# Attention, then routed experts, on one core: gathered token rows turned by a DMA on SyncE's queue, five places for expert weights, three evacuation tiles in the experts' first stage

## The chip, the cores and the metric

The kernel runs on one core of one Trainium2 chip, in one launch. The metric is the device time of one execution in microseconds (us); the figure for a kernel is the median of its runs.

## The reference

An attention over 8 batches of 8 heads (sequence 1152, head width 64) whose queries are averaged in pairs, so that 576 query rows per head remain, is followed by a routed two-layer network. All inputs and outputs are float32.

```
q_pool = q.reshape(B, H, S // 2, 2, D).mean(axis=3)
scores = scale * np.matmul(q_pool, k.transpose(0, 1, 3, 2))     # scale = 1/8
attn = exp(scores - max) / sum
x = (attn @ v), heads side by side                              # 4608 tokens x 512
for e in range(8):
    mask = domain_id == e
    out[mask] = np.maximum(x[mask] @ w1[e], 0.0) @ w2[e]         # 512 -> 1024 -> 512
```

## The kernel before

**Attention.** Two heads form a pair; there are 32 pairs of 12 steps, 384 steps in all (`for t in range(NST + 4)`, L849). A step computes 432 columns of key-by-query scores for both heads on TensorE (`score`, L578; matmul L587), and ScalarE takes their exponential into fp16 (`expo`, L593; L599). The weighted sums of values follow some steps later (`av`, L603; L610), and VectorE divides by the sums into the batch's tile `xb` (`evac`, L617; L624). A finished batch is written by DMA, row by row in token order, to a scratch tensor `x_tok` in memory (`put_x`, L634; nine pieces of 32 to 96 rows each, L639). All of these go on SyncE's queue (SP), except that of the last batch the pieces with odd `i` go on ScalarE's. The q loads (L99) are on SP too; the k and v loads, which cast to fp16 (L112, L121), the weight loads (L485 to L494), the gathers of token rows (L648) and the scatters of output rows (L504) are all on GpSimd's queue (POOL).

**Routing.** While the attention runs, VectorE works out each token's place in its expert's list. Every expert has room for 640 rows, five tiles of 128. The places are laid out so that an expert's tile 0 holds rows of the first two batches alone, tile 1 of the first four, tile 2 of the first six; tiles 3 and 4 may hold rows of any batch (`KO`, `IB`, `get_x` L653). So three tiles of every expert can be gathered before the last batch is done. There are 8 x 5 = 40 tiles.

**Expert tiles during the attention.** A tile costs four transposes of its gathered rows (`turn`, L747: L751, copied out by VectorE L756), 32 matmuls of the first stage (`up`, L763, relu on VectorE L768) and 8 of the second (`down`, L776, copied out L782). A planner (L907 to L921) hands out these pieces: each step has 769 ns (`STEP`); what the attention does in it is charged with C_S, C_AV, C_TK and C_TQ (370, 315, 460 and 420 ns), and a piece (240 ns for a turn, 216 ns for each of 4 matmuls up or 1 down) is issued when the running debt stays under 190 ns (`LAG`). No piece is begun by the planner from step NST - 5 = 379 on; at step NST + 1 a tile that was begun is finished (L896). `HELD` experts have their weights loaded during the attention, at the steps of `WANT`, into the places of `wpool`. `want` (L799) lists the gathers of the attention and the earliest step of each; 20 gathered tiles have room (`NFX`).

**Experts after the attention.** `plan_runs` (L831) makes a list of runs (expert, first tile, end). Before: expert 3 tiles 0 to 2; experts 0, 1, 2 from their first undone tile to 5; expert 3 tiles 3 and 4; experts 4 to 7, five tiles each. `first_xt` (L838) turns the first run's rows on TensorE (L843, L846). For each run (L1051), `stage1` (L996) multiplies the turned rows by the first weights, 128 hidden rows at a time (`f` = 0 to 7, L1010), and evacuates with relu, even `f` on ScalarE (L1015), odd `f` on VectorE (L1017). `stage2` (L1024) multiplies by the second weights (L1031) and copies out (L1037, L1039); then a scatter takes the 128 rows to the output. Between the tiles of `stage2`, `turn_tile` (L982; L985) transposes the next run's tiles on TensorE, and VectorE and ScalarE take turns in copying them out (L989, L991). When an expert is finished, the next unheld expert's weights are loaded into its place (L1066). In runs of up to four tiles two values of `f` share one PSUM tile, a half each:

```
            if m > 512:
                hp_ = hps.tile([P, 1024], FP32, name="hp")
            elif f % 2 == 0:
                hb_ = hps.tile([P, 1024], FP32, name="hp")
                hp_ = hb_[:, 0:512]
            else:
                hp_ = hb_[:, 512:1024]
```

The matmuls, copies and DMAs of each engine are executed in the order in which this program issues them. A block behind L1076, for experts with over 640 tokens, does not run on these inputs.

Of the kernel before, what the change touches and what calls it, by code (L numbers as in the profile page):

```python
# [9 lines left out]
P = 128  # L10
# [9 lines left out]
def kernel(  # L20
# [34 lines left out]
    NFX = 20  # L55
# [4 lines left out]
    wpool = ctx.enter_context(tc.tile_pool(name="wpool", bufs=4))  # L60
# [10 lines left out]
    idp = att.enter_context(tc.tile_pool(name="idp", bufs=2))  # L71
    lop = att.enter_context(tc.tile_pool(name="lop", bufs=6))
# [21 lines left out]
    def load_q(p, gate=False):  # L94
        b, h = p // HP, 2 * (p % HP)
        q2 = lds.tile([QP, 2, NJ, 2 * D], FP32, name="q2")
        mark(q2[0:1, 0, 0, 0:1], gate)
        for lo, hi in ((0, 1), (1, 2)) if p < 2 else ((0, 2),):
            nc.sync.dma_start(  # L99
                q2[:, lo:hi, :, :].rearrange("p h j d -> p h (j d)"),  # L100
                q[b, h + lo : h + hi].rearrange("h (p r) d -> p h (r d)", p=QP),
            )
        loaded.setdefault(p, {})["q2"] = q2
# [23 lines left out]
    k32 = perm.tile([P, 2, NC, D], FP32, name="k32")  # L127
# [12 lines left out]
    load_q(1)  # L140
# [23 lines left out]

    load_v(0)
    load_k(1)
    load_dom()
    keep_warm(17)
    make_identity(nc, ident[:, :])
# [258 lines left out]
    def id_group(g, i):  # L428
        if i == 0:
            gst["eq"] = idp.tile([P, GC, NH], F16, name="eq")  # L430
            nc.vector.tensor_tensor(
                out=gst["eq"][:, :, :],
                in0=hif[:, g * GC : (g + 1) * GC].unsqueeze(2).broadcast_to([P, GC, NH]),
                in1=iol[:, 0:NH].unsqueeze(1).broadcast_to([P, GC, NH]), op=ALU.is_equal,
            )
            gst[g] = idp.tile([P, GC, 2, NH], F16, name="hi2")
        else:
            nc.vector.tensor_tensor(
                out=gst[g][:, :, i - 1, :], in0=gst["eq"][:, :, :],
                in1=dig[:, i - 1, g * GC : (g + 1) * GC].unsqueeze(2).broadcast_to([P, GC, NH]),  # L440
                op=ALU.mult,
            )

    def id_lo(c):
        gst["lo", c] = lop.tile([P, P], F16, name="lo1")
# [95 lines left out]
    def new_kq(p):  # L541
        if p not in kq:
            kq[p] = work.tile([P, KW], F16, name="kq")
# [90 lines left out]
    def put_x(b, i):  # L634
        for lo, hi in zip(CUT, CUT[1:]):
            i_, m = (0, lo) if lo < 64 else (1 + (lo - 64) // P, (lo - 64) % P)
            if i_ == i:
                j, p0 = divmod(lo, QP)
                (nc.scalar if b == B - 1 and i % 2 else nc.sync).dma_start(  # L639
# [20 lines left out]
    xs = {}  # L660
    wqueue = []
# [10 lines left out]
    HELD = 4  # L672
    WANT = [66, 100, 134, 230]
# [34 lines left out]
    keep_warm(6)  # L708
# [3 lines left out]
    def rest_k():  # L712
        keep_warm(2)
# [3 lines left out]
        keep_warm(3)  # L717
# [23 lines left out]
    tiles, turned = [], []  # L741

    def add_tile(e, i):
# [3 lines left out]
        def turn():  # L747
            turned.append((e, i))
            mt = mpsum.tile([P, ND, P], F16, name="m")
            for cc in range(ND):  # L750
                nc.tensor.transpose(  # L751
                    mt[:, cc, :], in_=xs[e, i][:, cc * P : (cc + 1) * P], identity=ident16[:, :]
                )
            h0["xt"] = fill.tile([P, ND, P], F16, name="xt0")
            h0["h"] = fill.tile([P, NF, P], F16, name="h0")
            nc.vector.tensor_copy(h0["xt"][:, :, :], mt[:, :, :])  # L756

        def up(f):
            if f % 4 == 0:
                h0["m"] = mpsum.tile([P, 4, P], FP32, name="m")  # L760
# [12 lines left out]
        def down(f):  # L773
            if f == 0:
                h0["o"] = mpsum.tile([P, 512], FP32, name="m")
# [13 lines left out]
        fb.blocks.append(([turn], 240, 1, False, h0))  # L789
        fb.blocks.append(([lambda f=f: up(f) for f in range(4)], 216, 1, True, h0))  # L790
# [3 lines left out]
    for e, i in [(e, i) for i in range(2) for e in range(3)] + [  # L794
        (e, i) for e in range(3, HELD) for i in range(2)
    ]:
        add_tile(e, i)

    want = [(e, 0, 114) for e in range(3)] + [(e, 1, 212) for e in range(3)]  # L799
    want += [(e, i, 212) for e in range(3, E) for i in range(2)]  # L800
    want += [(e, 2, 308) for e in [3, 0, 1, 2] + list(range(HELD, E))]
# [27 lines left out]
    xt = {0: perm.tile([P, ND, CAP], F16, name="xt_first")}  # L829

    def plan_runs():  # L831
        early = [e for e in range(3, HELD) if done.get(e, 0) < NA]
        runs.extend((e, done.get(e, 0), NA) for e in early)
        runs.extend((e, done.get(e, 0), NTC) for e in range(3))
        runs.extend((e, NA if e in early else done[e], NTC) for e in range(3, HELD))
        runs.extend((e, 0, NTC) for e in range(HELD, E))

    def first_xt():  # L838
        e, i0, i1 = runs[0]
        for i in range(i0, i1):  # L840
            mt = mpsum.tile([P, ND, P], F16, name="m")
            for cc in range(ND):
                nc.tensor.transpose(  # L843
                    mt[:, cc, :], in_=xs[e, i][:, cc * P : (cc + 1) * P], identity=ident16[:, :]
                )
            nc.vector.tensor_copy(xt[0][:, :, (i - i0) * P : (i - i0 + 1) * P], mt[:, :, :])  # L846

    debt = 0
    for t in range(NST + 4):  # L849
# [17 lines left out]
        if t == 0:  # L867
            rest_k()
        if t in (1, 2, 3):
            keep_warm(3)  # L870
# [25 lines left out]
        if t == NST + 1:  # L896
# [3 lines left out]
            first_xt()  # L900
        if main and want and t >= want[0][2] and t >= last_get + 5 and not (t in later) and not mmq and not rq:
            e, i, _ = want[0]
            if len(got) < NFX or list(got)[len(got) - NFX] in turned:
                get_x(fxs, e, i)
                got[e, i] = last_get = t
                want.pop(0)
        while main:  # L907
            if fb.cur is None:
# [3 lines left out]
                if not b_[3] and t < got.get(b_[4]["xs"], NST) + 14:  # L912
# [51 lines left out]
    while wqueue:  # L964
# [4 lines left out]
        tc.tile_pool(name="hps", bufs=2, space=bass.MemoryType.PSUM, reuse_waits="tile")  # L969
# [4 lines left out]
    xps = ctx.enter_context(  # L974
        tc.tile_pool(name="xps", bufs=2, space=bass.MemoryType.PSUM, reuse_waits="tile")
    )
    tb = ctx.enter_context(tc.tile_pool(name="tb", bufs=2, reuse_waits="tile"))
    xsb = ctx.enter_context(tc.tile_pool(name="xsb", bufs=10, reuse_waits="tile"))
    xov = ctx.enter_context(tc.tile_pool(name="xov", bufs=1, reuse_waits="tile"))
    ob = ctx.enter_context(tc.tile_pool(name="ob", bufs=8, reuse_waits="tile"))  # L980

    def turn_tile(xt, x_, i):  # L982
        ps = xps.tile([P, ND, P], F16, name="xp")
        for cc in range(ND):
            nc.tensor.transpose(  # L985
                ps[:, cc, :], in_=x_[:, cc * P : (cc + 1) * P], identity=ident16[:, :]
            )
        if i % 2 == 0:
            nc.vector.tensor_copy(xt[:, :, i * P : (i + 1) * P], ps[:, :, :])  # L989
        else:  # L990
            nc.scalar.copy(xt[:, :, i * P : (i + 1) * P], ps[:, :, :])  # L991
# [4 lines left out]
    def stage1(w1h, xt, m, at=None):  # L996
        hT = tb.tile([P, NF, CAP], F16, name="hT")
        for f in range(NF):

            if m > 512:  # L1000
                hp_ = hps.tile([P, 1024], FP32, name="hp")
            elif f % 2 == 0:
                hb_ = hps.tile([P, 1024], FP32, name="hp")
                hp_ = hb_[:, 0:512]
            else:
                hp_ = hb_[:, 512:1024]
# [17 lines left out]
    def stage2(w2h, hT, n, ids, between=()):  # L1024
        between = list(between)
        for i in range(n):
            for _ in range(-(-len(between) // (n - i))):
                between.pop(0)()
# [22 lines left out]
    for k_, r in enumerate(runs):  # L1051
# [6 lines left out]
        get = lambda: fetch(k_ + 2)  # L1058
        h = stage1(wts[e][0], xt[k_], n * P, {1: get, 4: get, 6: get} if n < NTC else {1: get, 3: get, 5: get})
        btw = []  # L1060
        if k_ + 1 < len(runs):
            nx = xt[k_ + 1] = new_xt()
            en, j0, j1 = runs[k_ + 1]
            btw = [lambda i=i: turn_tile(nx, xs[en, j0 + i], i) for i in range(j1 - j0)]
        stage2(wts[e][1], h, n, lambda i, c=e * NTC + i0: gid[:, c + i : c + i + 1], btw)
# [10 lines left out]
    with tc.If(anyov > 0):  # L1076
# [9 lines left out]
        for e in range(E):  # L1086
# [4 lines left out]
            with tc.For_i(0, nt, 1) as j:  # L1091
# [13 lines left out]
                turn_tile(xto, xo, 0)  # L1105
# [30 lines left out]
```

The softmax here doesn't subtract the row's maximum and nothing guards it: scores larger than these inputs give would overflow.

## Time and profile before

| | |
|---|---|
| median of 4 runs | 473.52 us (471.48 to 474.54) |
| the profiled execution's own time | 473.74 us |
| its span in the profile | 471.7 us |
| ScalarE, first and last exponential | 9.32 us, end 317.05 us |
| last value matmul of the attention, end | 317.56 us |
| last matmul of all, end | 463.96 us |
| busy: TensorE, ScalarE, VectorE, GpSimd | 442.6, 347.6, 228.0, 160.4 us |

Times in the profile are in us from the start of the span unless marked ns. A row of groups names line, engine, operation, what it writes and reads, shapes and count; then busy time, mean ns of one, the idle time of the engine just before, and what ended that idle time. PE is TensorE's matmuls, PEld its weight loads, DVE VectorE, ACT ScalarE, SP SyncE's queue. The end of a matmul is modelled, so a group of matmuls is shown to end slightly after the next group has begun.

### The profile page before, as it was taken

Reading aid. Unit: us, or ns where it says so; the run is one execution under the profiler, and the core shown is the slowest. Engines: PE = TensorE matmul, PEld = TensorE weight load, DVE = VectorE, ACT = ScalarE, POOL = GpSimd, SP = SyncE. Lnnn points to the kernel's source line nnn. Section 1 sums busy time; section 2 is a strip of 40 time slices with the busy share of each in tenths; the row PEclk is TensorE's granted clock in tenths of the full one; section 3 lists DMA queues with packets and bytes.
Section 4 is the critical chain, followed back from the end, with each engine's and each line's share of the span. In section 5 each row is a group of like instructions: output and inputs, shape, how many; then the busy total and the mean of one; then the engine's idle time right before and its main releaser. Section 6 shows DMA issues by size and latency. Waiting matters only on the chain.

```text
span 471.7 us, 13280 instructions
## 1 busy us (share of the span) xinstructions
PE 442.6 (94%) x5683; PEld 313.6 (66%) x5683; DVE 228.0 (48%) x572; ACT 347.6 (74%) x459; POOL 160.4 (34%) x271
## 2 busy tenths in 40 slices
PE   7999999999999999999999999996888879999993
PEld 4777777777877877877787787773444445555551
DVE  4498778776555554655455554532223223232230
ACT  3999999999999999999999999981222223223220
POOL 4311141222511304564512441004335675532413
PEclk9999999999999999999999999998999999999998
DMA  9995699999999789599998676003219999912202
GB/s 205 219 243 93 119 242 223 182 259 198 157 243 243 114 190 206 99 195 265 241 154 206 140 124 143 1 25 107 78 68 165 212 218 228 236 46 84 89 20 98
DMA packets 48904, 75.23 MB, mean 159 GB/s; under 512 B 5567, under 2 KB 35008, under 8 KB 48834
## 3 DMA queue, kind: packets, MB, share of 16 engines
q0 software_dynamic: 35056, 50.05, 55.6%
q1 hardware_dynamic: 13186, 23.83, 18.8%
q8 instruction: 46, 0.75, 0.7%
q10 hardware_dynamic: 592, 0.39, 0.3%
q14 instruction: 24, 0.20, 0.1%
HBM read 95.46 MB, written 15.21 MB: 235 GB/s over the span
## 4 chain that ended last, share of the span: by engine, by line
ACT 54%; PE 23%; issue 10%; POOL 6%; DMA 3%; DVE 1%; POOLq 1%; SPq 0%; ACTq 0%
ACT e L599 52%; PE s L587 6%; PE hp L1010 6%; PE op L1031 4%; POOL out_dram L504 4%; PE acc L610 3%; DMA w2h<-in_moe_w_dram 3%; ACT hT L1015 2%; POOL xs L648 1%; PE m L763 1%; PE tp L550 1%; DMA x_tok<-xb 1%; PE xp L985 1%; SPq L639 0%; PE acc L161 0%
## 5 line engine op out<-in xcount | busy, mean ns | idle before, releaser
L599 ACT ACTIVATE e<-s 128x864 f16<-128x864 f32 x384 | 305.4, 893 | 2.8 <-PE s L587 2.4
L587 PE MATMUL s<-qz,kq 128*128 128x432 f16 (+2 forms) x1152 | 202.9, 284 | 4.1 <-ACT e L599 2.0
L610 PEld LDWEIGHTS <-e 128*128 128x128 f16 x2880 | 120.4, 97 | 24.9 <-DVE xb L624 8.2
L610 PE MATMUL acc<-v,e 128*128 128x65 f16 x2880 | 134.2, 193 | 0.3 <-ACT e L599 0.3
L587 PEld LDWEIGHTS <-kq 128*128 128x128 f16 x1152 | 97.5, 97 | 28.5 <-issue 8.1
L504 POOL DMA_INDIRECT out_dram<-osb,gid x40 | 40.1, 1002 | 101.5 <-ACT osb L1037 46.3
L1010 PE MATMUL hp<-xt,w1h 128*128 128x128 f16 (+3 forms) x384 | 57.7, 303 | 8.9 <-ACT hT L1015 8.9
L648 POOL DMA_INDIRECT xs<-x_tok,grow x40 | 41.6, 1040 | 71.1 <-DVE xs L92 55.2
L112 POOL DMA_DIRECT2D vs<-in_v_dram x32 | 23.9, 745 | 116.9 <-DVE v L529 55.5
L1031 PE MATMUL op<-w2h,hT 128*128 128x512 f16 x272 | 63.4, 379 | 0.0
L1010 PEld LDWEIGHTS <-w1h 128*128 128x128 f16 x416 | 35.9, 98 | 41.2 <-issue 17.5
L1015 ACT ACTIVATE hT<-hp 128x384 f16<-128x384 f32 (+2 forms) x36 | 20.7, 574 | 49.6 <-PE hp L1010 42.9
L1017 DVE TENSOR_SCALAR hT<-hp 128x384 f16<-128x384 f32 (+2 forms) x36 | 23.8, 661 | 65.2 <-PE hp L1010 65.2
L571 DVE COPY qz<-tp 64x576 f16<-64x576 f16 x62 | 28.2, 455 | 54.5 <-PE tp L564 50.5
L1037 ACT COPY osb<-op 128x512 f32<-128x512 f32 x21 | 12.3, 586 | 55.7 <-PE op L1031 50.0
L1031 PEld LDWEIGHTS <-hT 128*128 128x128 f16 x272 | 25.4, 98 | 25.2
L623 DVE RECIPROCAL rr<-acc 128x10 f32<-128x10 f32 x32 | 7.1, 221 | 46.6 <-PE acc L610 46.5
L520 DVE TENSOR_TENSOR qp<-q 96x768 f16<-96x768 f32 x31 | 29.3, 946 | 0.0
L624 DVE TENSOR_TENSOR xb<-acc,rr 128x640 f16<-128x640 f32 x32 | 26.4, 824 | 1.1
L1039 DVE COPY osb<-op 128x512 f32<-128x512 f32 x13 | 9.0, 692 | 35.5 <-PE op L1031 29.6
L121 POOL DMA_DIRECT2D k<-in_k_dram x31 | 23.3, 752 | 7.1 <-DVE q L92 4.1
L554 DVE COPY kq<-tp 128x1024 f16<-128x1024 f16 x31 | 21.2, 684 | 3.2 <-PE tp L550 3.2
(134 smaller groups left out, 324.7 us busy)
## 6 DMA issues: line engine op xcount, KB each, us to landing
q<-in_q_dram SPq DMA_DIRECT2D x30, 576.0 KB, 9.3
vs<-in_v_dram POOLq DMA_DIRECT2D x32, 288.0 KB, 6.1
k<-in_k_dram POOLq DMA_DIRECT2D x31, 288.0 KB, 8.5
w1h<-in_moe_w_dram POOLq DMA_DIRECT2D x16, 512.0 KB, 9.0
w2h<-in_moe_w_dram POOLq DMA_DIRECT2D x16, 512.0 KB, 12.1
x_tok<-xb SPq DMA_DIRECT2D x23, 96.0 KB, 4.1
x_tok<-xb SPq DMA_DIRECT2D x22, 64.0 KB, 4.6
q<-in_q_dram SPq DMA_DIRECT2D x4, 288.0 KB, 7.1
```

Of the source, the lines that this page charges most:

```text
L112: nc.gpsimd.dma_start(vs[:, :, :, :], v[b, h : h + 2].rearrange("h (p c) d -> p h c d", p=P))
L504: ins = nc.gpsimd.indirect_dma_start(out=dst[:, :], out_offset=bass.IndirectOffsetOnAxis(ap=ap, axis=0), in_=src, in_offset=None, **kw,)
L520: nc.vector.tensor_tensor(out=qp[:, :, :, :].rearrange("p j h d -> p h j d"), in0=q2[:, :, :, 0:D], in1=q2[:, :, :, D : 2 * D], op=ALU.add,)
L571: nc.vector.tensor_copy(qz[p % 2][r][lo : lo + 64, :], mt[lo : lo + 64, P : P + Sp])
L587: nc.tensor.matmul(s[:, r, o : o + n], lhsT=kq[p][:, c * P : (c + 1) * P], rhs=qz[p % 2][r][:, q0 : q0 + n], start=True, stop=True,)
L599: nc.scalar.activation(e_[:, :, o : o + W], st.pop(t)[:, :, 0:W], AF.Exp, bias=0.0, scale=0.0625)
L610: nc.tensor.matmul(acc[p][:, h, i * (D + 1) : (i + 1) * (D + 1)], lhsT=e_[:, h, o + QO[i] : o + QO[i] + P], rhs=v16[p % NV][:, c, h, 0 : D ...
L624: nc.vector.tensor_tensor(out=xb[b][:, :, 2 * hp * D : 2 * (hp + 1) * D].rearrange("p i (h d) -> p h i d", h=2), in0=a[:, :, :, 0:D], in1= ...
L648: nc.gpsimd.indirect_dma_start(out=dst, out_offset=None, in_=x_dram[0 : 1 + nb * Sp, :], in_offset=bass.IndirectOffsetOnAxis(ap=ap, axis=0),)
L1010: nc.tensor.matmul(hp_[:, lo : lo + n], lhsT=w1h[:, cc, f * P : (f + 1) * P], rhs=xt[:, cc, lo : lo + n], start=cc == 0, stop=cc == ND - 1,)
L1015: nc.scalar.activation(hT[:, f, 0:m], hp_[:, 0:m], AF.Relu)
L1031: nc.tensor.matmul(op_[:, :], lhsT=hT[:, f, i * P : (i + 1) * P], rhs=w2h[:, f, :], start=f == 0, stop=f == NF - 1,)
```

## The change

The turning of gathered rows goes from TensorE to a transposing DMA on SP's queue (`flip_x`), both for the tiles computed during the attention and for all runs after it. A tile of the attention is flipped 8 steps or more after its gather, and its first matmul may come 6 steps after the flip. `first_xt` is gone: the first run's three tiles are flipped during the attention into `xf`, which lies on the same place as the prologue's `k32`. After the attention, the flips of run k + 1 are issued on SP ahead of `stage1` of run k. The tiles planned for the attention are tiles 0, 1 and 2 of experts 0, 1 and 2.

`wpool` has five places, and the fifth expert's weights are loaded from step 290 on. The list of runs now begins with tiles 0 to 2 of expert 3 and of expert 4; then come experts 0, 1, 2, the rest of 3 and of 4, and experts 5 to 7. There are 14 places for rows gathered in the attention (before 20) and 16 for those after it (before 10).

`stage1` takes a PSUM tile of its own for every `f`, out of three; the two tiles that took the transposes are gone. All pieces of the last batch go to `x_tok` on SP. In the prologue, the second pair's q load and the load of `domain_id` are issued later, the identity is made before the first v and k loads, some filler matmuls (`keep_warm`) go, and the rest of the first keys is turned one step later. The routing's intermediate tiles (`eq`, `hi2`, `lo1`) use the buffers of the expert tiles in `fill`, `lo1` as eight slices of one tile, and `kq` has a pool of its own, with two buffers as before.

```diff
@@ -52,12 +52,12 @@
...
-    NFX = 20
+    NFX = 14
...
-    wpool = ctx.enter_context(tc.tile_pool(name="wpool", bufs=4))
+    wpool = ctx.enter_context(tc.tile_pool(name="wpool", bufs=5))
@@ -68,8 +68,7 @@
...
-    idp = att.enter_context(tc.tile_pool(name="idp", bufs=2))
-    lop = att.enter_context(tc.tile_pool(name="lop", bufs=6))
+    kqs = att.enter_context(tc.tile_pool(name="kqs", bufs=2))
@@ -95,7 +94,7 @@
...
-        for lo, hi in ((0, 1), (1, 2)) if p < 2 else ((0, 2),):
+        for lo, hi in ((0, 1), (1, 2)) if p == 0 else ((0, 2),):
@@ -124,7 +123,8 @@
...
-    k32 = perm.tile([P, 2, NC, D], FP32, name="k32")
+    xf = perm.tile([P, ND * CAP], F16, name="xf")
+    k32 = xf[:, 0 : 4 * NC * D].bitcast(FP32).rearrange("p (h c d) -> p h c d", h=2, c=NC)
@@ -137,7 +137,6 @@
...
-    load_q(1)
@@ -162,11 +161,10 @@
...
+    keep_warm(17)
+    make_identity(nc, ident[:, :])
     load_v(0)
     load_k(1)
-    load_dom()
-    keep_warm(17)
-    make_identity(nc, ident[:, :])
@@ -636,7 +636,7 @@
...
                 j, p0 = divmod(lo, QP)
-                (nc.scalar if b == B - 1 and i % 2 else nc.sync).dma_start(
+                nc.sync.dma_start(
@@ -658,6 +658,10 @@
...
+
+    def flip_x(dst, e, i):
+        nc.sync.dma_start_transpose(dst, xs[e, i][:, :])
+
...
     def want_weights(e):
...
-    HELD = 4
-    WANT = [66, 100, 134, 230]
+    HELD = 5
+    WANT = [66, 100, 134, 220, 290]
@@ -705,16 +709,16 @@
...
-    keep_warm(6)
+    load_q(1, True)
+    load_dom()
+    keep_warm(5)
...
     def rest_k():
-        keep_warm(2)
         kb = wps[:, 0, :].bitcast(F16)
         turn_k32(kb, CUTK, NC)
         nc.vector.tensor_copy(kq[0][:, CUTK * P : NC * P], kb[:, 0 : (NC - CUTK) * P])
-        keep_warm(3)
 
@@ -738,26 +742,27 @@
...
         def turn():
-            turned.append((e, i))
-            mt = mpsum.tile([P, ND, P], F16, name="m")
-            for cc in range(ND):
-                nc.tensor.transpose(
-                    mt[:, cc, :], in_=xs[e, i][:, cc * P : (cc + 1) * P], identity=ident16[:, :]
-                )
             h0["xt"] = fill.tile([P, ND, P], F16, name="xt0")
-            h0["h"] = fill.tile([P, NF, P], F16, name="h0")
-            nc.vector.tensor_copy(h0["xt"][:, :, :], mt[:, :, :])
+            flip_x(h0["xt"][:, :, :], e, i)
+            h0["t"] = now[0]
...
         def up(f):
+            if f == 0:
+                h0["h"] = fill.tile([P, NF, P], F16, name="h0")
+                begun.append((e, i))
+                turned.append((e, i))
             if f % 4 == 0:
@@ -786,19 +791,17 @@
...
-        fb.blocks.append(([turn], 240, 1, False, h0))
-        fb.blocks.append(([lambda f=f: up(f) for f in range(4)], 216, 1, True, h0))
+        turns.append((e, i, turn))
+        fb.blocks.append(([lambda f=f: up(f) for f in range(4)], 216, 1, False, h0))
         fb.blocks.append(([lambda f=f: up(f) for f in range(4, 8)], 216, 1, True, h0))
         fb.blocks.append(([lambda f=f: down(f) for f in range(NF)], 216, 1, True, h0))
 
-    for e, i in [(e, i) for i in range(2) for e in range(3)] + [
-        (e, i) for e in range(3, HELD) for i in range(2)
-    ]:
+    for e, i in [(e, i) for i in range(NA) for e in range(HELD - 2)]:
         add_tile(e, i)
...
-    want = [(e, 0, 114) for e in range(3)] + [(e, 1, 212) for e in range(3)]
-    want += [(e, i, 212) for e in range(3, E) for i in range(2)]
-    want += [(e, 2, 308) for e in [3, 0, 1, 2] + list(range(HELD, E))]
+    want = [(e, 0, 114) for e in range(HELD - 2)] + [(e, 1, 212) for e in range(HELD - 2)]
+    want += [(e, i, 212) for e in range(HELD - 2, E) for i in range(2)]
+    want += [(e, 2, 308) for e in [3, 4, 0, 1, 2, 5, 6, 7]]
@@ -826,24 +829,14 @@
...
     runs = []
-    xt = {0: perm.tile([P, ND, CAP], F16, name="xt_first")}
+    xt = {0: xf[:, :].rearrange("p (n c) -> p n c", n=ND)}
+    first = [(HELD - 2, i) for i in range(NA)]
 
     def plan_runs():
-        early = [e for e in range(3, HELD) if done.get(e, 0) < NA]
-        runs.extend((e, done.get(e, 0), NA) for e in early)
-        runs.extend((e, done.get(e, 0), NTC) for e in range(3))
-        runs.extend((e, NA if e in early else done[e], NTC) for e in range(3, HELD))
+        runs.extend((e, 0, NA) for e in (HELD - 2, HELD - 1))
+        runs.extend((e, done.get(e, 0), NTC) for e in range(HELD - 2))
+        runs.extend((e, NA, NTC) for e in (HELD - 2, HELD - 1))
         runs.extend((e, 0, NTC) for e in range(HELD, E))
-
-    def first_xt():
@@ -864,10 +857,8 @@
...
-        if t == 0:
+        if t == 1:
             rest_k()
-        if t in (1, 2, 3):
-            keep_warm(3)
@@ -897,19 +888,25 @@
...
             plan_runs()
-            first_xt()
...
+
+        if turns and t >= got.get(turns[0][:2], NST) + 8 and len(tiles) - len(turns) <= len(begun):
+            turns.pop(0)[2]()
+        if first and t >= got.get(first[0], NST) + 8:
+            e, i = first.pop(0)
+            turned.append((e, i))
+            flip_x(xt[0][:, :, i * P : (i + 1) * P], e, i)
...
                 b_ = fb.blocks[0]
-                if not b_[3] and t < got.get(b_[4]["xs"], NST) + 14:
+                if not b_[3] and t < b_[4].get("t", NST) + 6:
@@ -966,29 +963,15 @@
...
     hps = ctx.enter_context(
-        tc.tile_pool(name="hps", bufs=2, space=bass.MemoryType.PSUM, reuse_waits="tile")
+        tc.tile_pool(name="hps", bufs=3, space=bass.MemoryType.PSUM, reuse_waits="tile")
...
-    xps = ctx.enter_context(
-        tc.tile_pool(name="xps", bufs=2, space=bass.MemoryType.PSUM, reuse_waits="tile")
-    )
...
-    xsb = ctx.enter_context(tc.tile_pool(name="xsb", bufs=10, reuse_waits="tile"))
+    xsb = ctx.enter_context(tc.tile_pool(name="xsb", bufs=16, reuse_waits="tile"))
@@ -996,14 +979,7 @@
...
         for f in range(NF):
-
-            if m > 512:
-                hp_ = hps.tile([P, 1024], FP32, name="hp")
-            elif f % 2 == 0:
-                hb_ = hps.tile([P, 1024], FP32, name="hp")
-                hp_ = hb_[:, 0:512]
-            else:
-                hp_ = hb_[:, 512:1024]
+            hp_ = hps.tile([P, 1024], FP32, name="hp")
@@ -1055,14 +1028,14 @@
...
         if k_ == len(runs) - 1:
             nc.gpsimd.drain()
-        get = lambda: fetch(k_ + 2)
+        else:
+            xt[k_ + 1] = new_xt()
+            en, j0, j1 = runs[k_ + 1]
+            for j in range(j0, j1):
+                flip_x(xt[k_ + 1][:, :, (j - j0) * P : (j - j0 + 1) * P], en, j)
+        get = lambda: fetch(len(runs))
         h = stage1(wts[e][0], xt[k_], n * P, {1: get, 4: get, 6: get} if n < NTC else {1: get, 3: get, 5: get})
-        btw = []
-        if k_ + 1 < len(runs):
-            nx = xt[k_ + 1] = new_xt()
-            en, j0, j1 = runs[k_ + 1]
-            btw = [lambda i=i: turn_tile(nx, xs[en, j0 + i], i) for i in range(j1 - j0)]
-        stage2(wts[e][1], h, n, lambda i, c=e * NTC + i0: gid[:, c + i : c + i + 1], btw)
+        stage2(wts[e][1], h, n, lambda i, c=e * NTC + i0: gid[:, c + i : c + i + 1])
```

## The prediction

> **What bounds the kernel now.** I read the chain of waits first, then busy time by stage, then TensorE in order of time.
>
> ```profile
> ACT 54%; PE 23%; issue 10%; POOL 6%; DMA 3%; DVE 1%; POOLq 1%; SPq 0%; ACTq 0%
> L599 ACT ACTIVATE e<-s 128x864 f16<-128x864 f32 x384 | 305.4, 893 | 2.8 <-PE s L587 2.4
> ```
>
> ```profile
> 18.60:191.00 172.40, 169.77 (x2698) 133.11 (x2695) 115.60 (x317) 172.37 (x218) 44.00 (x65) 1.00 0.96 192
> 241.00:317.00 76.00, 75.08 (x1208) 59.47 (x1206) 36.32 (x80) 75.69 (x95) 16.82 (x29) 1.00 0.52 112
> 324.00:380.00 56.00, 47.19 (x266) 24.38 (x266) 14.01 (x35) 13.51 (x27) 28.22 (x49) 0.97 0.60 127
> 398.00:460.00 62.00, 62.00 (x411) 33.14 (x409) 19.22 (x32) 17.94 (x29) 22.39 (x43) 1.00 0.36 101
> ```
>
> The columns are the stretch, its length, busy us of PE, PEld, DVE, ACT, POOL, the clock, DMA share and GB/s. Up to 317 us ScalarE is busy without a break (172.37 of 172.40): the 384 exponentials set the pace, and it waits 2.8 us in all. After 324 it has little to do and TensorE sets the pace: 47 of 56 us busy at first, all of it later. So a saving on TensorE is worth nothing before 317 and everything after. TensorE in order of time:
>
> ```profile
> 317.39 1.89 PE L776 MATMUL m<-w2h,h 128*128 128x512 f16 x8
> 320.06 0.38 PE L843 MATMUL m<-ident,xs 128*128 128x128 f16 x4 [0.78 <-DVE osb L782]
> 322.75 0.81 PE L1010 MATMUL hp<-xt_first,w1h 128*128 128x384 f16 x4 [0.52 <-DVE xs L92]
> ...
> 339.46 1.46 PE L1010 MATMUL hp<-xt,w1h 128*128 128x384 f16 x8 [0.58 <-ACT hT L1015]
> 341.50 1.46 PE L1010 MATMUL hp<-xt,w1h 128*128 128x384 f16 x8 [0.58 <-ACT hT L1015]
> ...
> 379.86 0.60 PE L1010 MATMUL hp<-xt,w1h 128*128 128x256 f16 x4
> 380.99 1.03 PE L1010 MATMUL hp<-xt,w1h 128*128 128x256 f16 x8 [0.52 <-ACT hT L1015]
> ...
> 418.27 0.39 PE L985 MATMUL xp<-ident,xs 128*128 128x128 f16 x4
> 418.50 1.89 PE L1031 MATMUL op<-w2h,hT 128*128 128x512 f16 x8
> 420.22 0.39 PE L985 MATMUL xp<-ident,xs 128*128 128x128 f16 x4
> ```
>
> Three things are to be seen: work between the attention's end (317.55) and the first stage (322.75); a stop of 0.58 us ahead of every odd `f` in the runs of two and three tiles, which waits for ScalarE's copy of the other half of the same PSUM tile; and four transposes ahead of every tile of stage 2.
>
> **What the Trainium skill says.** "VectorE: DVE Perf Modes", The three transpose paths, gives 1309 ns for a 128x128 16-bit transpose by DMA and 390 ns on TensorE. A lone TensorE transpose is 219 ns here, and four in a row move the next matmul back by 0.23 us (418.27 to 418.50). "Advanced Engine Details and Errata", X-Bar Transpose (TRN2), says such DMAs "are as fast as regular DMAs"; "DMA: Bandwidth & Descriptors", Latency and other measured facts, gives 261 GB/s. No transposing DMA is in this trace, so neither is shown. The same page, Anatomy of one DMA, says that a wait for a semaphore is made by the issuing sequencer before dispatch. The trace agrees: SP waits 140.8 us in front of L639 for `xb`, and what is queued behind waits too.
>
> **The change part by part.** All in the tail unless said.
>
> Matmuls that stay. From pairs of rows above, 4 matmuls of 384 columns take 1.46 - 0.81 = 0.65 us, of 256 columns 0.43, and 8 of 512 take 1.73. A three-tile run: 8 x 0.65 + 3 x 1.73 = 10.4; two tiles: 3.44 + 3.46 = 6.9; five tiles: 8.69 (391.14 to 399.83) + 8.65 = 17.3. Walking the planner's loop with its own numbers, a step has on average 769 - (370 + 236 + 73) = 90 ns to spare; a tile costs 3696 before and 3456 after. Before, six tiles are done by the end, the sixth with 8 pieces left over: these are the eight L776 at 317.39. After, six again, the last piece at step 377; the seventh, though flipped, is too late to begin. So 34 tiles remain in both: 5 runs of three, 2 of two, 3 of five = 52.0 + 13.8 + 52.0 = 117.8 us. That the six are done earlier is worth nothing.
>
> Removed on TensorE:
> 1. the left-over pieces, 317.55 to 319.28: 1.7 us;
> 2. `first_xt`, 319.28 to 322.75: 3.5 us;
> 3. 31 x 0.22 us of transposes in stage 2: 6.8 us;
> 4. the stops ahead of odd `f`: eight matmuls of 384 columns recur every 2.04 us (339.46 to 341.50) where 1.30 would do, four times in four runs, 0.74 x 16 = 11.8; at 256 columns 1.50 against 0.86, four times, 2.6. With three own tiles, `f` + 3 needs what `f` left: ready after 0.65 + about 0.1 + 0.56 (L1017), well inside 3 x 0.65. Sum 14.4;
> 5. one slow pair at 324.14 (2.72 for 1.46): 1.3.
> Together 27.7; 117.8 + 27.7 = 145.5, and the tail measured is 463.96 - 317.55 = 146.4, so the account closes to 0.9.
>
> Evacuations keep up: VectorE and ScalarE are busy 19 and 18 of 62 us at 398 to 460. The end after the last matmul, 471.7 - 463.96 = 7.7, stays: last copy, last scatter, its landing.
>
> Weights: three experts instead of four are loaded in the tail, the first after run 3, at about 317 + 31 = 348; needed at 383. A load took 9 to 12 us to land: hidden. The fifth expert's load lies at steps 292 to 310, where the DMA share is 0.52: hidden.
>
> Gathers: 18 remain. Expert 0's tiles 3 and 4 need the last batch: `xb` at 318.7, nine pieces on SP at 0.57 (five took 2.86) until 323.8, landed by about 327, two gathers at 1.3 and 4.6 to land, about 334.8; their run begins at 338 or later: hidden, by 3 us. In the old order the second run already needed such rows.
>
> Attention: the flips wait on SP for gathers; behind them stand q loads. A q load lands in 9.3 us; the latest flip ahead of one (step 235 before step 240) leaves 13 steps to `prep_q`, some 10 us. Nothing. Six transposes and copies less on TensorE and VectorE: nothing, ScalarE is the bound.
>
> Start: ScalarE idles 1.36 us after its first exponential for the rest of the keys (L716). With two exponentials ahead of it most goes; but the later q load for pair 1 (issued about 8.3, 8 us to land) reaches `prep_q` about when that ran (16.79). I take 0.5 us gained, between 1.5 gained and 1 lost.
>
> **The unknown price** is one flip of 128x512: c us of the one queue's time. Below: 128 KB at 261 GB/s, 0.5 us. Above: four times 1309 ns, 5.2 us, if blocks follow one another. From this trace: queue 1's packets take 0.188 x 471.7 x 16 / 13186 = 0.108 us each; 128 KB in 1 KB packets is 8 per engine, 0.86 us, in 256 B packets 3.5 us. I take 1.5, with 2 us from the end of service to the semaphore (the shortest landings here are 1.5 for `x_tok` and 2.8 for gathers). Run 2's three flips stand on SP behind the nine pieces: 323.8 + 4.5 + 2 = 330.4, and run 1 is over at 317.55 + 10.4 = 327.9: a new wait of 2.5 us. Next tightest is the first five-tile run: its flips can begin when the second to last run has done stage 1, 3.5 + 6.9 = 10.4 us ahead; 7.5 + 2 fits.
>
> Sum: 317.55 - 0.5 + 117.8 + 2.5 + 7.7 = 445.1 span; the profiled execution has 2.0 outside its span, so **447 us**, against its own 473.7. That execution is within 0.1% of the median 473.5, so 447 stands for the median too.
>
> **The rivals.** Same sum, other c, the flips taken in order:
> - *Hidden but for run 2* (0.60): c up to 2. 444 at 0.5 us; at 2 us, run 2 waits 4 and the five-tile run 1.7: 450.
> - *A wait in place of the transposes* (0.24): c of 2 to 3.8, for instance because weight loads (228 GB/s and share 1.10 at 380 to 398) share the engines. At 3, run 2 waits 7.2 and the first five-tile run 6.7: 458. For it: SP's queue is one stream; against: the DMA share is 0.36 to 0.60 elsewhere.
> - *The DMA queue becomes the bound* (0.12), the case on the slow side: 31 flips follow one another from 324. At 5.2 us they end 162 us later; with the last run and the end, about 515. It decides from c = 3.9, where the sum reaches 473.5. The page's 1309 ns speaks for it, the other two places against.
> - *The attention gets longer* (0.04): flips or the late q load hold ScalarE by some 5 us: 452.
> - That the change doesn't do what it says: if stage 1 still stopped between halves, 14.4 us would stay, 461; I count it in the second case, as each `f` has its own tile.
>
> **Numbers.** Faster 0.86, same 0.02, slower 0.12; within 0.5% is about what a measurement of this kernel can tell from no change. The range leaves out the slow case and a little below: 442 (443 with 1.5 us gained at the start and c = 0.5, less 1 for the spread of the runs shown, 471.5 to 474.5) to 464 (c = 3.5).
>
> **What would show it.** Each step has its row: no L843 or L985; `hp` matmuls at a pitch of 0.65 us without "<-ACT hT"; first stage at about 317.5; a TensorE wait of 2 to 3 us ahead of run 2 and none after; the last exponential's end at 316.5. A flip that takes over 2 us of SP's queue, or gaps ahead of each five-tile run, would prove me wrong, as would a pace of exponentials above the present 0.79 us a step.

## The result and the profile after

The changed kernel takes 472.35 us (median of 34 runs, 466.63 to 475.32) against 473.2 us before (55 runs). The ratio is 0.9963, 95% interval 0.995 to 0.9975: 0.4% less, clear of 1, but inside the 0.5% that the prediction counts as no change. Runs over 1.5% above the fastest of their kernel are left out of the ratios and not of the medians. The forecast was 447 us, 5.6% less, and its range of 442 to 464 does not hold the time. The span of the profiled execution went from 471.7 to 469.6 us.

The same parts of the page as before, now of the changed kernel: the chain of waits and the groups of the exponentials and of the first stage.

```profile
ACT 52%; PE 18%; DMA 14%; issue 9%; POOL 4%; DVE 1%; POOLq 1%; SPq 0%; ACTq 0%
...
L599 ACT ACTIVATE e<-s 128x864 f16<-128x864 f32 x384 | 305.9, 893 | 7.1 <-PE s L587 6.7
...
L986 PE MATMUL hp<-xt,w1h 128*128 128x384 f16 (+3 forms) x384 | 60.4, 321 | 16.5 <-DMA xt<-xs 15.9
```

DMA was 3% of the chain and is 14%. ScalarE now waits 6.7 us for scores (2.4 before), and TensorE waits 15.9 us for turned rows. The tail (what follows the last value matmul) by stage, and TensorE in order of time:

```profile
354.00:382.00 28.00, 28.00 (x163) 15.65 (x160) 8.24 (x24) 8.30 (x17) 19.71 (x34) 1.00 1.06 187
382.00:395.00 13.00, 8.94 (x49) 5.49 (x48) 2.39 (x5) 2.12 (x5) 3.54 (x5) 0.87 1.28 196
395.00:419.00 24.00, 12.20 (x65) 6.23 (x66) 2.48 (x3) 3.40 (x5) 8.04 (x16) 0.72 1.32 161
419.00:462.00 43.00, 43.00 (x250) 21.41 (x247) 11.57 (x15) 10.32 (x16) 14.06 (x27) 1.00 0.36 99
```

```profile
321.70 0.81 PE L986 MATMUL hp<-xf,w1h 128*128 128x384 f16 x4
323.03 4.72 PE L986 MATMUL hp<-xf,w1h 128*128 128x384 f16 x28 [0.52 <-DVE xb L624]
327.60 5.34 PE L1004 MATMUL op<-w2h,hT 128*128 128x512 f16 x24
333.53 5.36 PE L986 MATMUL hp<-xt,w1h 128*128 128x384 f16 x32 [0.59 <-issue]
...
375.04 3.66 PE L986 MATMUL hp<-xt,w1h 128*128 128x256 f16 x32
378.54 3.62 PE L1004 MATMUL op<-w2h,hT 128*128 128x512 f16 x16
386.18 5.33 PE L986 MATMUL hp<-xt,w1h 128*128 128x256 f16 x32 [4.03 <-DMA xt<-xs]
391.35 3.62 PE L1004 MATMUL op<-w2h,hT 128*128 128x512 f16 x16
404.49 1.86 PE L986 MATMUL hp<-xt,w1h 128*128 128x512 f16 x4 [9.53 <-DMA xt<-xs]
408.67 10.42 PE L986 MATMUL hp<-xt,w1h 128*128 128x128 f16 x60 [2.31 <-DMA xt<-xs]
```

Everything that was to be removed is gone: 32 matmuls of 384 columns follow one another without a stop (5.36 us, and 5.34 for a whole stage 2), and stage 1 begins as the attention's last matmuls end. For 60 us the tail goes as forecast. Then, between 382 and 418.9, TensorE stands three times for turned rows, while the weights of experts 6 and 7 are being loaded, and its clock column falls to 0.87 and 0.72. Runs are numbered from 1 below: the second two-tile run is run 7, the first five-tile run is run 8.

The account, in us:

| | before | forecast | after |
|---|---|---|---|
| exponential of step 12 begins (start of the kernel) | 20.98 | 0.5 earlier | 19.27 |
| last exponential ends | 317.05 | 316.5 | 321.37 |
| tail, last value matmul to last matmul | 146.4 | 120.3 | 140.5 |
| last matmul to the end of the span | 7.7 | 7.7 | 7.2 |

So two things are left to explain: some 20 us in the tail, and an attention that ends 4.3 us later although it began 1.7 us earlier, 6 us lost on the way.

### The profile page after: what moved, and what is told of

It is laid out like the page before. It is cut to its first block, busy times and chain, and to the rows that moved or that the text cites. A ratio compares the mean times of both kernels' runs of the same rounds, so it can differ in the third digit from the quotient of the medians.

```text
span 469.6 us, 12969 instructions
## 1 busy us (share of the span) xinstructions
PE 433.4 (92%) x5508; PEld 305.7 (65%) x5508; DVE 218.1 (46%) x549; ACT 342.7 (73%) x451; POOL 160.4 (34%) x271
## 4 chain that ended last, share of the span: by engine, by line
ACT 52%; PE 18%; DMA 14%; issue 9%; POOL 4%; DVE 1%; POOLq 1%; SPq 0%; ACTq 0%
ACT e L599 52%; DMA w2h<-in_moe_w_dram 9%; PE hp L986 5%; PE s L587 4%; PE op L1004 4%; DMA xf<-xs 3%; POOL out_dram L504 3%; DMA q<-in_q_dram 2%; PE acc L610 2%; PE m L768 1%; DVE qp L520 0%; PE tp L550 0%; POOLq L1030 0%; PE tp L564 0%; POOL gap L502 0%
## 5 line engine op out<-in xcount | busy, mean ns | idle before, releaser
L986 PE MATMUL hp<-xt,w1h 128*128 128x384 f16 (+3 forms) x384 | 60.4, 321 | 16.5 <-DMA xt<-xs 15.9
L986 PEld LDWEIGHTS <-w1h 128*128 128x128 f16 x416 | 38.6, 103 | 44.8 <-issue 17.1
L991 ACT ACTIVATE hT<-hp 128x384 f16<-128x384 f32 (+2 forms) x40 | 21.3, 534 | 53.6 <-PE hp L986 53.4
L1004 PE MATMUL op<-w2h,hT 128*128 128x512 f16 x272 | 60.3, 379 | 0.0
L1004 PEld LDWEIGHTS <-hT 128*128 128x128 f16 x272 | 26.5, 98 | 30.4
L120 POOL DMA_DIRECT2D k<-in_k_dram x31 | 23.3, 750 | 7.6 <-DVE q L91 4.3
```

Of the source, the lines that this page charges most:

```text
L986: nc.tensor.matmul(hp_[:, lo : lo + n], lhsT=w1h[:, cc, f * P : (f + 1) * P], rhs=xt[:, cc, lo : lo + n], start=cc == 0, stop=cc == ND - 1,)
L1004: nc.tensor.matmul(op_[:, :], lhsT=hT[:, f, i * P : (i + 1) * P], rhs=w2h[:, f, :], start=f == 0, stop=f == NF - 1,)
```

## The experiments

**Is it the weights that slow the flips?** (A flip is one transposing DMA of 128 rows.) The first kernel takes away the other transfer, not the flips:

```diff
-            fns, wts[er] = load_w(er)
-            for fn in fns:
-                fn()
+            wts[er] = wts[e]
```

> The changed kernel, but the weights of experts 5, 6 and 7 are not loaded after the attention: their runs multiply by the weights of the expert that was just finished (the loading of three experts' weights is left out). Theory, sharing: a flip is 512 packets of 256 bytes and is slow only where it alternates on the DMA engines with the large packets of a weight load. Then every flip of the tail takes about 1.2 to 1.3 us of SP's queue and lands in about 4 us, TensorE waits nowhere more than 1 us for turned rows, and the tail shrinks from 140.7 to about 119 us: some 450 us. Rival, order: the flips are late because SP runs them in order behind gathers and behind the two places for turned rows. Then the waits ahead of the second two-tile run and of the first five-tile run stay, 10 us or more together: 460 us or more.

Measured: 451.4 us, ratio to before 0.955 (0.950 to 0.959). The view of the flips' line in the tail, first of the changed kernel ahead of the loads and beside them, then of this one:

```profile
L663 SPq DMA_TRANSPOSE xt<-xs x14: 1190/1216/1307, 327.8 to 361.0; - x14
...
DMA to landing us min/median/max: 4.0/4.1/4.2
```

```profile
L663 SPq DMA_TRANSPOSE xt<-xs x10: 1190/4187/5288, 380.0 to 419.1; - x10
...
DMA to landing us min/median/max: 15.5/17.2/18.9
```

```profile
L663 SPq DMA_TRANSPOSE xt<-xs x31: 1188/1219/1639, 326.1 to 401.5; - x31
...
DMA to landing us min/median/max: 2.4/3.5/4.6
```

The columns are ns of SP's queue for one issue (least, median, most) and the time to landing, of those flips whose landing the trace tells (two of the ten beside the loads). Without the loads all 31 flips take 1.2 to 1.6 us and the profile has no wait for turned rows; beside the loads the median issue is over 4 us, and the two landings are 15.5 and 18.9. Order alone is out as the cause: the places for turned rows and the order on SP are the same in both. So are late gathers: from 360 to 418 us SP waited for one only once, for 0.9 us.

**Where the attention lost its time.** In the changed kernel one edit, the step at which expert 3's weights are loaded:

```diff
-    WANT = [66, 100, 134, 220, 290]
+    WANT = [66, 100, 134, 170, 290]
```

> The changed kernel with expert 3's weights loaded from step 170 on in place of step 220, so that they do not lie beside the flips of steps 220 to 240. Theory, sharing: the flip that took 15.0 us at 201.33 lands in about 4 us, the q load behind it is no longer late, ScalarE loses no time at steps 252 to 264, and the last exponential ends about 6 us earlier: some 466 us, with the tail as before. Rival, gathers: the flip is slow because of the gathers around it and the q load is late on any account: the stall stays and the time is within 1.5 us of 472.4.

Measured: 465.98 us, ratio 0.982 (0.977 to 0.987); the last exponential begins at 314.19 where the changed kernel has 320.44. The time is as expected, and the stall of steps 252 to 264 is gone, but its first part came from a link ahead of the one that I named. SyncE's queue in the changed kernel, what it waited for in 195 to 230 us, and VectorE's wait that followed:

```profile
182.98 0.58 SPq L98 DMA_DIRECT2D q<-in_q_dram  x1
199.37 1.19 SPq L663 DMA_TRANSPOSE xf<-xs  x1
200.67 0.55 SPq L98 DMA_DIRECT2D q<-in_q_dram  x1
201.33 1.21 SPq L663 DMA_TRANSPOSE xf<-xs  x1
```

```profile
SPq L663 <- DMA xs<-x_tok,grow: 15.7, 1, 15.7
```

```profile
212.79 0.95 DVE L520 TENSOR_TENSOR qp<-q 96x768 f16<-96x768 f32 x1 [5.88 <-DMA q<-in_q_dram]
```

The flip stood at the head of SP for 15.7 us until its gather (issued by GpSimd at 189.12) landed, only at about 199.3, beside the weight load; with the load moved, the same gather is issued at 189.04 and lands at 193.34, and the flip stands for 9.8 us, which costs nothing. The q load behind the flip so left at 200.67 and was 5.9 us late for VectorE; between steps 252 and 264 ScalarE fell from 1.6 us ahead of the kernel before to 4.6 behind. The second, smaller wait (1.5 us at 222.58) has the cause that was expected: the next flip took 15 us to land, and the q load behind it went out as it landed.

**The parts by themselves.** Turning back on TensorE after the attention, the rest of the change kept; stage 1 has two tiles then, as two go to the transposes:

```diff
-        tc.tile_pool(name="hps", bufs=3, space=bass.MemoryType.PSUM, reuse_waits="tile")
+        tc.tile_pool(name="hps", bufs=2, space=bass.MemoryType.PSUM, reuse_waits="tile")
...
+            btw = [lambda i=i: turn_tile(nx, xs[en, j0 + i], i) for i in range(j1 - j0)]
```

> The changed kernel, but after the attention the rows are turned on TensorE as before (two PSUM tiles for it, two for stage 1, still one for each f); flips during the attention stay. Theory, sharing: the tail is 117.8 us of matmuls + 6.8 us of transposes + about 1 to 2 us of starts, 126 us in place of 140.7: some 457 us. Rival, weights: without the slow flips the late weights themselves become the wait (the three loads share the DMA engines with gathers), and run 7 still waits some 8 us or more: 465 us or more.

Measured: 461.5 us, 0.976 (0.972 to 0.981): faster than with flips, although TensorE does more, and 4.5 above the expectation. The reason stands in its profile, beside the lines of the changed kernel shown above (5.36 and 3.66 us for 32 matmuls):

```profile
343.99 5.90 PE L1000 MATMUL hp<-xt,w1h 128*128 128x384 f16 x32
...
378.53 4.43 PE L1000 MATMUL hp<-xt,w1h 128*128 128x256 f16 x32
```

With two tiles stage 1 is 0.5 us longer in each of five three-tile runs and 0.8 in two two-tile runs (4.43 against 3.66), 4.1 in all. The third tile is worth that: the last version below has four tiles beside the same transposes and is back at 5.36. No run waited for weights.

The kernel before with a tile of its own for every `f` and nothing else:

```diff
-            if m > 512:
-                hp_ = hps.tile([P, 1024], FP32, name="hp")
-            elif f % 2 == 0:
-                hb_ = hps.tile([P, 1024], FP32, name="hp")
-                hp_ = hb_[:, 0:512]
-            else:
-                hp_ = hb_[:, 512:1024]
+            hp_ = hps.tile([P, 1024], FP32, name="hp")
```

> The kernel before with one edit: a PSUM tile of its own for every f in stage 1 (two of them, as many as before). Theory: the stops ahead of odd f were the false sharing of one tile, and all 14.4 us that the prediction gave to them are gained: 459 us. Rival: with two tiles the stop only moves from the odd f to f + 2 or into the copies, and less than half is gained: 466 us or more.

Measured: 461.9 us, 0.974 (0.969 to 0.978): 11.9 of the 14.4 us. No stop is left ahead of odd `f`:

```profile
349.05 5.89 PE L1003 MATMUL hp<-xt,w1h 128*128 128x384 f16 x32
```

Four runs of three tiles at 0.5 and one of two at 0.8 are some 2.8 us short of the changed kernel's, which has the third tile. This one edit is worth more than the whole change.

**Would more lead do?** Four places for turned rows, with expert 3's weights early:

```diff
-        return tb.tile([P, ND, CAP], F16, name="xt")
+        return xtp.tile([P, ND, CAP], F16, name="xt")
...
+    xtp = ctx.enter_context(tc.tile_pool(name="xtp", bufs=4, reuse_waits="tile"))
```

> The changed kernel with expert 3's weights from step 170 on, and four places for turned rows in place of two, so that SP may flip further ahead of TensorE. Theory, sharing with bandwidth by packet: the second two-tile run's rows are flipped ahead of the second weight load and its wait of 4.2 us goes; the first five-tile run's last two rows are gathered at about 356 to 358, so its five flips still lie beside the weight loads at 4 to 5 us each and end only about 385 to 390, and some 4 to 8 of its 16 us of waiting and slow clock remain: 454 to 460 us. Rival, places: only the two places held the flips back, they all go ahead of the loads: 450 us or less. Second rival, the loads only: what bounds is the sum of bytes beside the weights, the flips are late as before: 464 us or more.

Measured: 458.9 us, 0.970 (0.967 to 0.972), as expected. The wait ahead of the second two-tile run is gone, but ahead of the first five-tile run more is left than I had said: 11.5 us of waiting where I gave 4 to 8 for waiting and slow clock together.

```profile
376.14 3.66 PE L987 MATMUL hp<-xt,w1h 128*128 128x256 f16 x32
379.63 3.62 PE L1005 MATMUL op<-w2h,hT 128*128 128x512 f16 x16
393.46 1.87 PE L987 MATMUL hp<-xt,w1h 128*128 128x512 f16 x4 [10.21 <-DMA xt<-xs]
396.60 10.28 PE L987 MATMUL hp<-xt,w1h 128*128 128x128 f16 x60 [1.27 <-DMA xt<-xs]
```

TensorE reached this run 7 us sooner than with two places (383.1 against 390.2), but its flips began only at 366.6, behind one that waited for its gather, and lay under the same loads.

**Bytes or packets?** Expert 3's weights early, and the late weights in pieces of 256 columns, so 512 bytes a row:

```diff
+            for lo in range(0, F, 256):
+                nc.gpsimd.dma_start(
+                    wts[er][0][:, :, lo : lo + 256],
+                    moe_w1[er][:, lo : lo + 256].rearrange("(c p) f -> p c f", p=P),
+                )
```

(and the second weights likewise)

> The changed kernel with expert 3's weights from step 170 on, and the late weights of experts 5, 6 and 7 loaded in pieces of 256 columns (512 bytes a row in place of 1024 and 2048), the same bytes in six DMAs in place of four. Theory, packets take turns: a flip's 32 packets on each engine each wait for one packet of the weight load, so with packets of a half to a quarter of the size SP's issue of a flip beside the loads falls from 4 to 5 us to 2 to 3 us, although the loads themselves last longer; the waits ahead of the second two-tile and the first five-tile run shrink, 466 us becomes 455 to 462. Rival, bytes: the flips are slow because the loads take the bandwidth, so the size of the packets changes nothing or makes it worse: flips stay at 4 us or more and the time at 465 us or more.

Measured: 464.1 us, 0.976 (0.971 to 0.980). The flips' line beside the loads, first of the kernel with expert 3's weights early and large packets, then of this one:

```profile
L663 SPq DMA_TRANSPOSE xt<-xs x8: 2836/4502/5187, 375.7 to 407.0; - x8
...
  PE hp L986: 10.9, 2
```

```profile
L663 SPq DMA_TRANSPOSE xt<-xs x10: 1191/1588/4163, 382.0 to 400.5; - x10
...
  PE hp L986: 0.2, 1
```

The median issue falls from 4.5 us to 1.6, and TensorE waits 0.2 us for turned rows where it waited 10.9. That wait alone proves little, since TensorE now waited 3.1 us for the first weights of run 8 as well. But from the first flip of this run to the matmul that waited for the last one it is 18.6 us in place of 30.5. Nor did the loads give way: by the packets of the traces, the second and third late load took 19.6 and 27.3 us from first issue to last packet, against 23.3 and 25.6 with large packets. So it is the size of the neighbour's packets, not their bytes, that made the flips dear (that a load is six DMAs in place of four was not tried apart).

The time is above the expected 455 to 462, and with four runs on another chip it is not told apart from that of the early weights alone (0.977 to 0.987). Besides the 3.1 us TensorE stopped for some 8.5 us in the tail: half of it at places for which the profile names no cause, half for copies of stage 1 that came late.

**Both causes away.** Expert 3's weights early and no late weights:

> The changed kernel with both causes away at once: expert 3's weights from step 170 on, and no weight loads after the attention (experts 5, 6 and 7 multiply by the weights of the expert just finished, so the loading of three experts' weights is left out). Theory: the two losses are separate and add up, 472.4 - 21 - 6.4 = 445 us, and nothing else stands between the forecast of 447 and the measured time. Rival, overlap: the earlier end of the attention brings the first flips and the last batch's writes closer together and some of the gain is lost at run 2: 448 us or more.

Measured: 453.6 us (ratio to before 0.952, 0.947 to 0.956), not 445, with the kernel before at 476.4 in the same comparison. (The loading of three experts' weights is left out here, as in the first experiment.) Its TensorE stopped in the tail for 2.5, 0.9 and 0.9 us, in places where the run with small packets stopped too and no other run did, and its attention was 2.9 us later than in the repetition below. So I ran the base and the three kernels made from it on one chip.

> The changed kernel itself, as the base of four that run on one chip: with and without the late weight loads, expert 3's weights at step 220 or at 170. 0.996 of the kernel before.

> Second of the four: expert 3's weights from step 170 on. Theory (two separate losses): 6.4 us less than the base, as on the other chip.

> Third of the four: no weight loads after the attention (left out: the loading of three experts' weights). Theory: 21 us less than the base, as on the other chip.

> Fourth of the four: both edits (left out: the loading of three experts' weights). Theory: the losses are separate and add, 27 us less than the base, and the 453.6 us of the first run of this kernel come from its chip, where TensorE stopped four times in the tail for nothing that the profile names. Rival: the kernel itself makes these stops, since the attention ends earlier: 22 us less or under.

| expert 3's weights | late weights loaded | us | ratio to before |
|---|---|---|---|
| step 220 | yes (the change) | 473.45 | 0.995 (0.992 to 0.998) |
| step 170 | yes | 466.56 | 0.988 (0.984 to 0.991) |
| step 220 | no | 452.15 | 0.958 (0.954 to 0.963) |
| step 170 | no | 444.62 | 0.940 (0.937 to 0.943) |

The two losses are 6.9 and 21.3 us alone and 28.8 together. The base spreads widely, from 466.8 to 476.0; by the median of the runs that its ratio uses, 471.5, they are 4.9, 19.3 and 26.8. So they are separate and add up to within 3 us, and the rival of overlap (22 us or less together) is out. The last kernel's tail has no wait for turned rows:

```profile
368.88 3.66 PE L986 MATMUL hp<-xt,w1h 128*128 128x256 f16 x32
...
375.82 3.66 PE L986 MATMUL hp<-xt,w1h 128*128 128x256 f16 x32
...
382.77 8.86 PE L986 MATMUL hp<-xt,w1h 128*128 128x512 f16 x64
```

What made the stops in the first run of this kernel stays open; on this chip the same kernel does not make them.

**A version that beats both.** Expert 3's weights early; flips only for runs 2 to 5, before the loads weigh on them, TensorE for the later runs; five-tile runs cut in three and two, which makes room for four tiles of stage 1 beside two for transposes:

```diff
+        runs.extend((e, a, b) for e in range(HELD, E) for a, b in ((0, NA), (NA, NTC)))
...
+            hp_ = hps.tile([P, 512], FP32, name="hp")
...
+            for j in range(j0, j1) if k_ < 4 else ():
```

> A version drawn from the runs so far: expert 3's weights from step 170 on; flips for the runs that are turned before the first late weight load matters (runs 2 to 5), transposes on TensorE for all later ones; the five-tile runs are cut into three and two tiles, so that a tile of stage 1 needs half the PSUM and there are four of them beside two for transposes. Theory: no wait for turned rows, stage 1 without stops, tail = 117.8 + 22 x 0.22 + 1.4 = 124 us after an attention that ends at 315.5: 449 us, faster than both kernels. Rival: the late weights become the wait once the runs before them are shorter: run 8 waits for w1h, 455 us or more.

Measured: 449.5 us, 0.951 (0.948 to 0.954). It keeps all loads and all of the work.

```profile
363.62 0.39 PE L982 MATMUL xp<-ident,xs 128*128 128x128 f16 x4
363.84 1.89 PE L1021 MATMUL op<-w2h,hT 128*128 128x512 f16 x8
...
384.25 5.36 PE L1000 MATMUL hp<-xt,w1h 128*128 128x384 f16 x32
389.45 0.39 PE L982 MATMUL xp<-ident,xs 128*128 128x128 f16 x4
```

Where the flips cost the changed kernel some 20 us, TensorE pays 0.22 us a tile (363.62 to 363.84). The parts of this version were not tried one by one.

## Why the prediction was wrong

**What held.** ScalarE bounds the attention and TensorE the tail. The 27.7 us of work and stops are removed, and the matmuls that stay cost 117.8 us: with the loads out of the way (last row of the table) the same kernel takes 444.6 us against the 447 of the sum. The 2.4 between them are small terms: the start gained 1.7 in place of 0.5, run 2 waits 0.6 to 0.9 in place of 2.5, and a stop of 0.5 in run 1 was not in the sum. A flip alone was sized about rightly: 1.5 us of the queue and 2 to the semaphore were taken, 1.2 to 1.3 and a landing 2.4 to 4.6 after the issue are measured.

**The step that failed in the tail** is "Weights: [...] hidden", together with the single price of a flip, c = 1.5 us of the queue and 2 to land, for all 31. The sum had 2.5 us of waiting for turned rows, all at run 2; measured are 0.6 us there and 15.9 at runs 7 and 8. The weights do land in time, and I asked only that. I did not ask what they do to what flies beside them. Three late loads begin at 356, 369 and 390, and the flips of runs 7 and 8 fall among them. c is 1.2 to 1.3 us up to 380 and 2.6 to 5.3 from 381 to 417, and the landings that the trace tells between 370 and 406 are 11.5 to 18.9 us. Run 7 waits for the landing alone (its two flips were issued in 1.2 and 1.3 us and landed after 11.5 and 13.9), run 8 for both. TensorE stands for 4.2, 9.7 and 2.3 us (from 382.0 to 386.18, from 394.8 to 404.49, and the wait in the profile), and with the waits its clock falls (0.72 at 395 to 419) and the two first stages are 1.7 and 3.4 us longer; with 1.3 us at runs 1 and 2 that is 22.6, and 117.8 + 22.6 = 140.4 of the 140.5 measured. The mechanism was on the list as the second rival, with chance 0.24, and even with its cause, but with one c of 2 to 3.8 everywhere; and the place that the sum called next tightest ("7.5 + 2 fits") is where most is lost. That the time hardly moved is a coincidence of sizes: 27.7 us saved in the tail and 1.7 at the start, against 22.6 and 6 lost.

Why a neighbour costs so much is read from the packets, on the page of each kernel:

```profile
DMA packets 48904, 75.23 MB, mean 159 GB/s; under 512 B 5567, under 2 KB 35008, under 8 KB 48834
```

```profile
DMA packets 71192, 80.60 MB, mean 172 GB/s; under 512 B 27855, under 2 KB 57296, under 8 KB 71122
```

The second is the changed kernel: 22,288 more packets under 512 bytes with 41 flips, about 544 each for 128 KB. The trace's own list has 512 packets of 256 bytes for every flip, and the rest are of 4 bytes. The prediction's 3.5 us from queue 1's packets was for this size; alone a flip takes a third of that, beside the loads 2.6 to 5.3, and I chose one price without asking what packets there are. The Trainium skill, "DMA: Bandwidth & Descriptors", Queues, rings and completion order, says that each DMA engine takes turns between the queues that have work for it, a packet at a time. I had not used it. A packet of that page holds several descriptors, and no run here shows whether the packets of the trace are the same. The run with small weight packets agrees: same bytes, and the flip's issue falls from 4.5 to 1.6 us. And the DMA share that I set against this rival, 0.36 to 0.60, is that of other stretches: at 376 to 404 it was 1.13 before, most of it from the loads.

**The step that failed in the attention** is "the flips wait on SP for gathers; behind them stand q loads. [...] Nothing." The reasoning had the right queue. It took the median of 9.3 us for the q load and gave the flip's wait for its gather no time of its own. At that place expert 3's weights are loaded, and the prediction asked only where the fifth expert's are: the gather took about 10 us, the q load 12. The 10 us of slack were used up, and 6 us lost; the case was given 0.04 and "some 5 us".

**The sign and the slow case.** The kernel is 0.4% faster, which by the prediction's own words is about what can't be told from no change, so it does not bear out the forecast that it gets faster. The case in which the DMA queue bounds the whole tail did not come: after 419 there is no wait.

## What to carry to other kernels

Moving work from a full engine to a DMA queue is not done when the transfer is priced alone: price it beside each transfer that will fly at that time, and look at the packets of both, since here a stream of small packets beside large ones took over three times as long. A transfer that waits for another one holds everything that stands behind it in its queue; count that with the landings at that place, not with the median. And look first for the cheap edit in the same stage: here a tile of its own for every evacuation gave 12 us without any transfer.

## What the runs showed of the hardware

- A transposing DMA of 128x512 16-bit elements from SBUF to SBUF takes 1.2 to 1.3 us of SP's queue, in a few cases 1.6, and 2.4 to 4.6 us to land when no weight load runs. Beside one the flips from 381 to 417 us take 2.6 to 5.3 us, mostly 4 to 5, and those from 370 to 406 land after 11.5 to 18.9. Alone the flips of a five-tile run start 1.31 us apart (377.20 to 382.45 in the first run without late loads), and 1.2 of it is the issue: 128 KB in 1.31 us, about 100 GB/s. The Trainium skill ("DMA: Bandwidth & Descriptors", Latency and other measured facts) gives 261 GB/s, the prediction's lower bound for c; flips of this size do not reach it.
- Both sides lose. The last piece of a late load lands after 19.2 and 21.3 us beside the flips (issued at 373.72 and 394.68), and after 11.7 to 12.4 in the kernel before. All DMA together moved less, over 376 to 404 us (changed kernel first, then before; the last three columns are TensorE's clock, DMA share, GB/s):

```profile
376.00:404.00 28.00, 14.94 (x89) 9.23 (x87) 4.78 (x13) 4.02 (x10) 12.67 (x22) 0.87 1.32 158
```

```profile
376.00:404.00 28.00, 25.59 (x183) 14.87 (x182) 7.87 (x19) 8.75 (x16) 16.99 (x28) 1.00 1.13 221
```

- TensorE's granted clock fell to 0.72 in the stage with waits of 2 to 10 us (395 to 419), and is 1.00 at these times in the first run without late loads and in the last version. That the one causes the other was not tried by itself.
